# Short filler matmuls in the front, and the loads of two sequence steps cut in two by partitions

## The chip, the core and the metric

The kernel runs on one core of one Trainium2 chip, as one launch. The metric is the device time of that launch in microseconds: the median over several runs, with all seven inputs in device memory at the start and the output back in device memory at the end.

Five engines work side by side and each follows its own list of instructions: TensorE (PE in the profile, with its weight loads as a row of their own, PEld), VectorE (DVE), ScalarE (ACT), GpSimd (POOL) and SyncE (SP). Sixteen DMA engines move data. SP and POOL only issue transfers to them.

## The reference, cut to what matters

A gated recurrence over 768 tokens, for 4 batches and 8 heads of width 48, and after it a two-layer network with a product of two projections:

```python
f = 1.0 / (1.0 + np.exp(-f_logit))
for t in range(S):
    state = f[:, :, t, :, None] * state + np.einsum('bhd,bhe->bhde', k[:, :, t], v[:, :, t])
    y[:, :, t] = np.einsum('bhd,bhde->bhe', q[:, :, t], state)
x = y.transpose(0, 2, 1, 3).reshape(B * S, H * D)       # 3072 x 384
gate = np.maximum(x @ w_gate, 0.0)                      # 384 -> 1536
out = (gate * (x @ w_val)) @ w_out                      # 1536 -> 384
```

`q`, `k`, `v` and `f_logit` are 4 x 8 x 768 x 48 in float32, so for one head the 48 numbers of a token (192 bytes) lie together, and the tokens of a head follow one another.

## The kernel before

**Tiling.** The sequence is cut into six steps of 128 tokens (`C = 128`, `NC = 6`), and the batches of a step go in two pairs. Within a step the recurrence is a masked product of queries and keys plus a carried state (one 48 x 48 block for each head and batch). For each step and pair the kernel:

- loads f, k, q and v, one transfer each (`load`, issued at line 487 on SP);
- takes exp and ln of f on ACT (lines 742 and 744; 585 and 586 in the first two steps), sums over tokens with a triangular matmul (751; 594 in the first two steps), and takes two exponentials of the sums (761 and 763; 608);
- multiplies k and q by them ("hats", lines 773 and 777 on POOL; 610);
- transposes the hats, as DMA transposes issued by SP (795) from step 2 on, and on TensorE (642) in the first two steps;
- forms scores (817; 667), masks them on DVE (827; 683), multiplies with v and with the carried state (852; 712 and 717), and copies the result into `xT` (881; 729);
- updates the state (900; 692), and runs the network over the 512 rows of the step: two projections (922), relu on ACT (928), product on DVE (932), the output projection (965), a copy (975), and a store issued by SP (979).

Steps 0 and 1 (`twos`) take two neighbouring tokens into one partition, so their loads are 128 partitions of 8 runs of 384 bytes. From step 2 on the loads are 128 partitions (tokens) of 16 runs (heads of two batches) of 192 bytes.

**What sets the order.** Every instruction is added to a list with an assumed cost, and a planner (`Plan.schedule`, with `settle` for eight rounds) walks it and fixes the order on each engine before the program is emitted. On the chip each engine follows its list in order and waits on semaphores. A transfer has a semaphore of its own for each buffer slot, and its reader waits for 16 counts for each transfer of the slot so far (`dma`, line 460). In the planner a load is a number of parts (`64 * (b1 - b0)`) of 13.5 or 23 ns. All loads, transposes and stores go through SP's one queue in list order. The nine weight loads (three parts each of `wg`, `wv`, `wo`) go through POOL's queue (line 508), and the last of `wo` stands in POOL's list behind hats and copies of step 1. SP holds a load back until the load three before it has landed (`flight = 3`).

**Filler matmuls.** Until the first loads are in, TensorE has nothing to do. The kernel fills gaps in TensorE's planned list up to planned time 15 us with matmuls on a tile of zeros, into a bank of PSUM that is kept free until then (lines 1013 to 1036). `zeros` is 128 x 512 and is cleared by DVE (line 447) before the first of them. The number in a gap follows from the planned length of the gap:

```python
        gap, each = op.start - at, 0.44 if at < 4.0 else 0.23
        if begun and op.start <= warm_until:
            for _ in range(int((0.9 if gap > 1.5 else 0.6) * gap / each)):
                busy.append((op, warm))
```

This gives 18 matmuls of 512 columns: one before the gaps are counted (line 1015) and 17 at line 1024, which stand as 1 ahead of the `pick` matmul (434), 7 ahead of the first sums (594), 6 ahead of the first transposes (642), 1 ahead of the first scores (667) and 2 ahead of the first products with v (712). Every one loads its weights anew, so a matmul is two instructions in TensorE's list.

Of the kernel before, what the change touches and what calls it, by code (L numbers as in the profile page):

```python
# [8 lines left out]
BF16 = mybir.dt.bfloat16  # L9
# [33 lines left out]
class Plan:  # L43
# [10 lines left out]
    def add(self, eng, emit, reads=(), writes=(), occ=0.5, lat=0.2, prio=0, opens=(), after=(), follows=()):  # L54
        op = Op(eng, emit, list(reads), list(writes), occ, lat, prio, opens, after, follows)
        op.idx = len(self.ops)
        self.ops.append(op)
        return op
# [244 lines left out]
def bass_hgrn2_outer__then__ffn_reglu_kernel(  # L303
# [8 lines left out]
    out: bass.AP,  # L312
):
    twos = (0, 1)
    pe_hats = {(0, 0), (0, 1), (1, 0), (1, 1)}
    by_pool = {(0, 0, 0, 1), (0, 1, 0, 1)}
    halves = {0: 6, 1: 4, 2: 6}
# [9 lines left out]
    B, H, S, D = q.shape  # L327
    C = 128
# [12 lines left out]
    sb = nc.alloc_sbuf_tensor  # L341
# [40 lines left out]
    mask2 = sb("mask2", [128, 2, 2, 64], BF16)  # L382
    ident = sb("ident", [128, 128], BF16)
    ones = sb("ones", [128, 1], BF16)
    zeros = sb("zeros", [128, 512], BF16)
    banks = [nc.alloc_psum_tensor(f"ps{i}", [128, 512], F32) for i in range(8)]

    pl = Plan({"bc": 2, "bc4": 4, "tp": 2, "s": 4, "y": 2, "kv": 2, "f": 4})
    add = pl.add
    gp, ve, sc, te, sy = nc.gpsimd, nc.vector, nc.scalar, nc.tensor, nc.sync  # L390
# [13 lines left out]
    def pool_t(n):  # L404
        return dict(occ=0.1 + n * 2.2 / 1000.0, lat=0.12)
# [7 lines left out]
    def fill(eng, name, ap, value, cols, prio, key=None):  # L413
        e = engine[eng]
        add(eng, lambda: e.memset(ap, value), [], [key or name], occ=0.07 + cols / (1090.0 if eng == "DVE" else 1020.0), prio=prio)
# [19 lines left out]
    for t, name, src, sname in ((upto, "upto", tri, "tri"), (below, "below", tris, "tris")):  # L435
        add("DVE", lambda t=t, src=src: ve.tensor_tensor(t[:], src[:], same.ap[:, 0:128], ALU.mult), [same, sname], [name],
            occ=0.25, prio=-19)
    add("DVE", lambda: ve.tensor_copy(pick2[:], same.ap[:, 0:128].rearrange("p (b t) -> p b t", b=2)[:, :, 0]), [same], ["pick2"],
        occ=0.1, prio=-19)
    for i, src, name in ((0, upto, "upto"), (1, below, "below"), (1, upto, "upto")):  # L440
        lo = [m for m in range(2) if not (i and (name == "upto") != (m == 1))]
# [2 lines left out]
            src[:, 64:128].unsqueeze(1).to_broadcast([128, len(lo), 64]), ALU.add), [name], [f"mask2_{i}{m}" for m in lo],  # L444
            prio=-9, **pool_t(64 * len(lo)))

    fill("DVE", "zeros", zeros[:], 0.0, 256, -30)
    for i in range(NB):
        fill("DVE", f"bneg{i}", bneg[:, i], 0.0, 512, -28 if i < 1 else 11 if i < 2 else 30)
    for i in range(NH):  # L450
# [9 lines left out]
    def dma(op, slot, flow, parts, n=1):  # L460

        if slot not in slots:
            slots[slot] = [nc.alloc_semaphore(f"d_{slot}"), 0]
        slots[slot][1] += 16 * n
        op.sem, op.goal = slots[slot]
        op.flow, op.parts = flow, (n * parts[0], *parts[1:])

    srcs = {"f": f_logit, "k": k, "q": q, "v": v}

    def slot_of(n, c, pr):  # L470
        return (2 * c + pr) % NL[n]

    def in_keys(n, c, b0, b1):
        return [f"{n}{slot_of(n, c, b // 2)}_{b % 2}" for b in range(b0, b1)]

    def load(n, c, b0, b1, after=()):
        last = tails.get("load")
        t = ld[n]
        both, one = c in twos, b1 - b0 == 1
        if both:  # L480
            src = bass.AP(tensor=srcs[n].tensor, offset=(2 * c + b0 // 2) * H * S * D, ap=[[2 * D, C], [S * D, H], [1, 2 * D]])
            dst = bass.AP(tensor=t, offset=slot_of(n, c, b0 // 2) * 2 * HD, ap=[[NL[n] * 2 * HD, 128], [2 * D, H], [1, 2 * D]])
        else:
            src = bass.AP(tensor=srcs[n].tensor, offset=b0 * H * S * D + c * C * D,
                          ap=[[D, C], [S * D, (b1 - b0) * H], [1, D]])
            dst = t[:, slot_of(n, c, b0 // 2), b0 % 2:b0 % 2 + b1 - b0, :, :].rearrange("p b h d -> p (b h) d")
        op = add("SP", lambda: sy.dma_start(dst, src), [], in_keys(n, c, b0, b1),  # L487
                 occ=0.45 if both else 0.7 if one else 1.0, lat=0.9, prio=c * 100, after=after,
                 follows=[last] if last else [])
        tails["load"] = op  # L490
        dma(op, f"{n}{slot_of(n, c, b0 // 2)}" + f"_{b0 % 2}" * one, 0.95 * (b1 - b0),
            (64, 19, 27, 2.4) if both else (64 * (b1 - b0), 13.5, 23))
        return op

    WJ = NJ // wsteps
# [2 lines left out]
    def load_w(nm, s, after):  # L498
        if nm == "wo":
            src = bass.AP(tensor=w_out.tensor, offset=s * WJ * 128 * DM,  # L500
                          ap=[[DM, 128], [128 * DM, WJ], [1, DM]])
            dst = wo[:, s * WJ:(s + 1) * WJ, :]
        else:
            src = bass.AP(tensor=wsrc[nm].tensor, offset=s * WJ * 128,
                          ap=[[DFF, 128], [128 * DFF, NK], [1, WJ * 128]])
            dst = (wg if nm == "wg" else wv)[:, :, s * WJ * 128:(s + 1) * WJ * 128]
        last = tails.get("load_w")
        op = add("POOL", lambda: gp.dma_start(dst, src), [], [f"{nm}{s}"], occ=0.8, lat=1.2, prio=50, after=after,
                 follows=[last] if last else [])
        tails["load_w"] = op  # L510
        dma(op, f"{nm}{s}", 2.45, (32, 62, 80, 2.2) if nm == "wo" else (24, 80, 80, 2.6))
        return op

    loads, done, firsts = [], {}, []
    for item in first:
        item, _, behind = item.partition("@")
        gate = [done[behind]] if behind else []
        if item[0] == "w":
            op = load_w(item[:2], int(item[2:]), gate)
        else:  # L520
            c, b = int(item[1]), int(item[3])
# [464 lines left out]
    for c in range(NC):  # L986
        for b in range(0, B, 2):
            for n in "fkqv":
                if f"{n}{c}.{b // 2}" not in done:
                    loads.append(load(n, c, b, b + 2, loads[-flight:][:1]))  # L990
        for b in range(0, B, 2):
            if c in twos:
                attention_pair(c, b)
            else:
                attention_front(c, b)
                attention_front(c, b + 1)
                attention(c, (b, b + 1))
        for b0, b1, js in groups.get(c, [(0, 4, range(NJ))]):
            len0, js = len(pend), list(js)
            for at, j in enumerate(js):  # L1000
                ffn_hidden(c, b0, b1, j)
                if pend and c > 0 and (len(js) - 1 - at) / len(js) * len0 < len(pend):
                    ffn_out(*pend.pop(0))
            if c > 0 and js[-1] == NJ - 1:
                pend += [(c, [b]) for b in range(b0, b1)]
        if c == 0:
            for b in range(0, B, 2):
                ffn_out(0, [b, b + 1])
    for item in pend[:-1]:
        ffn_out(*item)  # L1010
    ffn_end(NC - 1, B - 1, [(0, 256), (256, DM)])

    WARM = 512
    warm_until = 15.0
    add("PE", lambda: te.matmul(banks[-1][:, 0:WARM], zeros[:, 0:128], zeros[:, 0:WARM]), ["zeros"], ["warm"], occ=0.2,
        prio=-30)
    for e in pl.ENGINES:
        pl.free0[e] = 0.8
    spare = banks[-1]
    order = pl.settle([(bk, warm_until if bk is spare else 0.0) for bk in banks], rounds=8, early=set(firsts))  # L1020
    waits = pl.needs()

    def warm():
        return te.matmul(spare[:, 0:WARM], zeros[:, 0:128], zeros[:, 0:WARM], start=True, stop=True, skip_group_check=True)

    busy, at, begun = [], pl.free0["PE"], False
    for op in order["PE"]:
        gap, each = op.start - at, 0.44 if at < 4.0 else 0.23
        if begun and op.start <= warm_until:
            for _ in range(int((0.9 if gap > 1.5 else 0.6) * gap / each)):  # L1030
                busy.append((op, warm))
        begun = True
        at = op.start + op.occ
    fillers = {}
    for op, emit in busy:
# [2 lines left out]
    for e in ("PE", "ACT", "DVE", "POOL"):  # L1038
        n = 0
# [75 lines left out]
```

## Time and profile before

| | before |
|---|---|
| time, median of 3 runs | 193.62 us (192.35 to 194.12) |
| span of the profiled run | 190.5 us |
| PE busy | 183.2 us, 96% |
| DVE, ACT, POOL busy | 105.1, 109.5, 76.2 us |
| moved by DMA | 32.04 MB in 108854 packets |
| of it on SP's queue | 28.19 MB in 104848 packets |
| f, k, q and v loads, issue to landing (median) | 5.6, 5.6, 5.1, 5.4 us |

A DMA share of 1.00 in the tables by stage means that on average each of the 16 engines had one packet under way; it goes over 1 where packets of one engine overlap. In a list of instructions the first number is the start from the beginning of the span, the second the time, "x16" the number of instructions merged into the line, and what stands in brackets is the idle time of the engine ahead of it and what ended that.

### The profile page before, as it was taken

To read this page: it belongs to the slowest core of one execution; us is meant where nothing else is said; L and a number is where in the kernel's file an instruction comes from. 1 tells how busy PE (TensorE), PEld (TensorE's weight loads), DVE (VectorE), ACT (ScalarE), POOL (GpSimd) and SP (SyncE) were. 2 spreads that over 40 slices of the span, in tenths; PEclk is the share of its full clock that TensorE was granted. 3 is DMA by queue.
4 is the path that set the end of the run, shared out by engine and by line. 5 is a ranking of instruction groups with operands and counts; after the bars stand their busy time and mean duration, and the time that the engine had idled before them with its cause. 6 is when DMAs were issued, how large, how long until landed. Compare 5 with 4: busy or idle time off the path is not lost.

```text
span 190.5 us, 5030 instructions
## 1 busy us (share of the span) xinstructions
PE 183.2 (96%) x2079; PEld 108.1 (57%) x2079; DVE 105.1 (55%) x189; ACT 109.5 (57%) x244; POOL 76.2 (40%) x109
## 2 busy tenths in 40 slices
PE   7988799999999999999999999999999999999995
PEld 2457584556685466768545564454555555554564
DVE  7699465994555866518695374625538233343300
ACT  3775459735698486575967739466533533334322
POOL 8497404771376638445393473715400000000000
PEclk9999999999999999999999999999999999999999
DMA  6999999999999999999999998999640310011113
GB/s 164 323 264 203 192 298 237 200 230 195 256 215 154 222 162 223 252 193 252 158 217 141 208 217 167 229 195 229 124 114 29 86 41 27 14 45 41 41 53 112
DMA packets 108854, 32.04 MB, mean 168 GB/s; under 512 B 101792, under 2 KB 108832, under 8 KB 108832
## 3 DMA queue, kind: packets, MB, share of 16 engines
q1 hardware_dynamic: 104848, 28.19, 73.2%
q0 software_dynamic: 3984, 3.54, 11.9%
q8 instruction: 16, 0.26, 0.6%
q14 instruction: 6, 0.05, 0.1%
HBM read 25.95 MB, written 4.72 MB: 161 GB/s over the span
## 4 chain that ended last, share of the span: by engine, by line
PE 73%; DMA 13%; ACT 4%; DVE 3%; SPq 2%; POOL 2%; issue 2%
PE ps L922 41%; PE ps L965 19%; DMA f_in<-in_f_logit_dram 8%; DMA wo<-in_moe_w_out_dram 5%; PE ps L852 2%; PE ps L817 2%; PE ps L751 1%; DVE qkT L650 1%; POOL hats L610 1%; PE ps L594 1%; SPq L487 1%; PE ps L900 1%; PE ps L945 1%; PE ps L667 1%; ACT f_in L742 1%
## 5 line engine op out<-in xcount | busy, mean ns | idle before, releaser
L932 DVE TENSOR_TENSOR gT<-relu,ps 128x512 bf16<-128x512 bf16 (+1 forms) x88 | 51.0, 587 | 61.2 <-PE ps L922 38.3
L928 ACT ACTIVATE relu<-ps 128x512 bf16<-128x512 f32 (+1 forms) x88 | 45.4, 521 | 27.6 <-PE ps L922 27.2
L922 PE MATMUL ps<-xT,wv 128*128 128x512 bf16 (+1 forms) x264 | 61.2, 340 | 0.0
L922 PE MATMUL ps<-xT,wg 128*128 128x512 bf16 (+1 forms) x264 | 61.1, 340 | 0.0
L965 PE MATMUL ps<-wo,gT 128*128 128x384 bf16 x276 | 49.0, 326 | 0.3 <-DMA wo<-in_moe_w_out_dram 0.3
L965 PEld LDWEIGHTS ps<-wo,gT 128*128 128x128 bf16 x276 | 26.2, 98 | 18.3 <-DMA wo<-in_moe_w_out_dram 0.4
L922 PEld LDWEIGHTS ps<-xT,wg 128*128 128x128 bf16 x264 | 24.8, 98 | 19.7 <-issue 1.6
L922 PEld LDWEIGHTS ps<-xT,wv 128*128 128x128 bf16 x264 | 25.0, 98 | 19.2
L975 ACT ACTIVATE osb<-ps 128x384 f32<-128x384 f32 x23 | 11.2, 494 | 26.2 <-PE ps L965 26.2
L827 DVE TENSOR_TENSOR ptm<-ps,tri 128x512 bf16<-128x512 f32 x32 | 20.4, 682 | 5.3 <-PE ps L817 5.2
L773 POOL TENSOR_TENSOR hats<-k_in,expo 128x384 bf16<-128x384 f32 x16 | 15.8, 998 | 17.7 <-ACT expo L761 15.3
L570 POOL TENSOR_TENSOR st<-ssum,dec 128x384 bf16<-128x384 f32 x16 | 13.1, 832 | 23.0 <-DVE ssum L568 22.9
L777 POOL TENSOR_TENSOR hats<-q_in,expo 128x384 bf16<-128x384 f32 x16 | 15.7, 998 | 4.4 <-DMA q_in<-in_q_dram 4.3
L568 DVE TENSOR_TENSOR ssum<-ps,st 128x384 f32<-128x384 f32 x16 | 8.4, 552 | 3.7 <-PE ps L900 3.5
L683 DVE TENSOR_TENSOR ptm<-ps,mask 128x512 bf16<-128x512 f32 x14 | 8.7, 680 | 1.5 <-PE ps L667 1.5
L761 ACT ACTIVATE expo<-ps 128x384 f32<-128x384 f32 x16 | 7.9, 494 | 2.8 <-PE ps L754 2.7
L763 ACT ACTIVATE expo<-ps 128x384 f32<-128x384 f32 x16 | 8.0, 501 | 0.0
L807 POOL CAST vpad<-v_in 128x384 bf16<-128x384 f32 x16 | 7.6, 507 | 0.4 <-DMA v_in<-in_v_dram 0.2
L742 ACT ACTIVATE f_in<-f_in 128x768 f32<-128x768 f32 x8 | 6.7, 842 | 1.5 <-DMA f_in<-in_f_logit_dram 1.5
L729 ACT ACTIVATE xT<-ps 128x384 bf16<-128x384 f32 x8 | 4.2, 599 | 5.8 <-PE ps L717 5.8
L744 ACT ACTIVATE bneg<-f_in 128x768 bf16<-128x768 f32 x8 | 6.7, 843 | 0.1
L881 ACT ACTIVATE xT<-ps 128x384 bf16<-128x384 f32 x12 | 5.2, 486 | 2.5 <-PE ps L852 2.5
(85 smaller groups left out, 163.4 us busy)
## 6 DMA issues: line engine op xcount, KB each, us to landing
f_in<-in_f_logit_dram SPq DMA_DIRECT2D x12, 384.0 KB, 5.6
k_in<-in_k_dram SPq DMA_DIRECT2D x12, 384.0 KB, 5.6
q_in<-in_q_dram SPq DMA_DIRECT2D x12, 384.0 KB, 5.1
v_in<-in_v_dram SPq DMA_DIRECT2D x12, 384.0 KB, 5.4
out_dram<-osb SPq DMA_DIRECT2D x23, 192.0 KB, 2.4
wg<-in_moe_w_gate_dram POOLq DMA_DIRECT2D x3, 384.0 KB, 5.5
wv<-in_moe_w_val_dram POOLq DMA_DIRECT2D x3, 384.0 KB, 6.2
wo<-in_moe_w_out_dram POOLq DMA_DIRECT2D x3, 384.0 KB, 8.8
```

Source lines behind the costliest of these rows:

```text
L568: add("DVE", lambda: ve.tensor_tensor(tmp[:, :], kv.ap[:, 0:HD], s_old[:, :], ALU.add), [kv, f"S{b}_{(c + 1) % 2}"], [key], prio=P + 8, ** ...
L570: add("POOL", lambda: gp.tensor_tensor(t4(s_new), t4(tmp), rate, ALU.mult), [key] + dk, [f"S{b}_{c % 2}"], prio=P + 8, **pool_t(HD))
L683: add("DVE", lambda i=i, j=j, mask=mask: ve.tensor_tensor(ptm[ms[i]][:, j, :, :], s[i][j].ap[:, :].rearrange("p (n t) -> p n t", n=NP), ma ...
L742: add("ACT", lambda: sc.activation(fl, fl, AF.Exp, scale=-1.0), keys, keys, prio=P, **act_t(2 * HD))
L773: add("POOL", lambda: gp.tensor_tensor(hk, kin[:, b % 2, :, :], ex[:, 1, :].rearrange("p (h d) -> p h d", h=H), ALU.mult), in_keys("k", c, ...
L777: add(e, lambda: engine[e].tensor_tensor(hq, qin[:, b % 2, :, :], ex[:, 0, :].rearrange("p (h d) -> p h d", h=H), ALU.mult), in_keys("q", ...
L827: add("DVE", lambda mi=mi, j=j, s=s: ve.tensor_tensor(ptm[mi][:, j, :, :], s.ap[:, :].rearrange("p (n t) -> p n t", n=NP), mask, ALU.mult) ...
L922: mm = te.matmul(bank.ap[:, 0:n], wt[:, kt, j * 128:(j + 1) * 128], xT[xi][:, kt, n0:n1], start=(kt == 0), stop=(kt == NK - 1))
L928: add("ACT", lambda: sc.activation(relu[ri][:, 0:n], gate.ap[:, 0:n], AF.Relu), [gate], [f"relu{ri}"], prio=P, **act_t(n))
L932: add("DVE", lambda: ve.tensor_tensor(gT[gi][:, j, n0:n1], relu[ri][:, 0:n], val.ap[:, 0:n], ALU.mult), [val, f"relu{ri}"], [f"gT{gi}_{j}_ ...
L965: mm = te.matmul(o[b].ap[:, 0:DM], gT[gi][:, j, b * C:(b + 1) * C], wo[:, j, :], start=(j == 0), stop=(j == NJ - 1))
L975: add("ACT", lambda b=b, oi=oi: sc.activation(osb[oi][:, :], o[b].ap[:, 0:DM], AF.Copy), [o[b]], [f"osb{oi}"], prio=P, **act_t(DM))
```

## The change

Two edits that have nothing to do with each other.

**Fillers.** The formula is replaced by a list written out. The first five gaps over 0.4 us in TensorE's planned list get 18 matmuls of 64 columns, 58 of 64, and 8, 3 and 5 of 128. The first matmul is 128 columns wide in place of 512. That is 93 matmuls in place of 18. They stand at the same five places. `zeros` shrinks to 128 x 128, so its clearing does too. The purpose is to keep TensorE's array busy with pieces that are short, so that a filler never holds up a real matmul for long.

**Loads.** Each f, k, q and v load of steps 3 and 4 becomes two transfers, over partitions 0 to 119 and 120 to 127 for f, 0 to 103 and 104 to 127 for k, 0 to 71 and 72 to 127 for q, 0 to 87 and 88 to 127 for v. Both are issued one after the other in the place of the one, on the same semaphore, and the reader waits for 32 counts. The bytes and the runs of 192 bytes are the same. The purpose is to spread the transfers differently over the DMA engines.

The order of the instructions on PE, DVE, ACT and POOL is otherwise that of before, apart from three clearings of `dec` on DVE that move together. On SP it is that of before with 16 more transfers.

```diff
+    parted = (3, 4)
...
-    zeros = sb("zeros", [128, 512], BF16)
+    zeros = sb("zeros", [128, 128], BF16)
...
-    fill("DVE", "zeros", zeros[:], 0.0, 256, -30)
+    fill("DVE", "zeros", zeros[:], 0.0, 64, -30)
...
         if both:
...
+            ends = [(src, dst)]
         else:
-            src = bass.AP(tensor=srcs[n].tensor, offset=b0 * H * S * D + c * C * D,
-                          ap=[[D, C], [S * D, (b1 - b0) * H], [1, D]])
-            dst = t[:, slot_of(n, c, b0 // 2), b0 % 2:b0 % 2 + b1 - b0, :, :].rearrange("p b h d -> p (b h) d")
-        op = add("SP", lambda: sy.dma_start(dst, src), [], in_keys(n, c, b0, b1),
+            cut = (0, {"f": 120, "k": 104, "q": 72, "v": 88}[n], C) if c in parted else (0, C)
+            ends = [(bass.AP(tensor=srcs[n].tensor, offset=b0 * H * S * D + c * C * D + lo * D,
+                             ap=[[D, hi - lo], [S * D, (b1 - b0) * H], [1, D]]),
+                     t[lo:hi, slot_of(n, c, b0 // 2), b0 % 2:b0 % 2 + b1 - b0, :, :].rearrange("p b h d -> p (b h) d"))
+                    for lo, hi in zip(cut, cut[1:])]
+        op = add("SP", lambda: [sy.dma_start(dst, src) for src, dst in ends], [], in_keys(n, c, b0, b1),
...
-            (64, 19, 27, 2.4) if both else (64 * (b1 - b0), 13.5, 23))
+            (64, 19, 27, 2.4) if both else (64 * (b1 - b0) // len(ends), 13.5, 23), len(ends))
...
-    WARM = 512
-    warm_until = 15.0
-    add("PE", lambda: te.matmul(banks[-1][:, 0:WARM], zeros[:, 0:128], zeros[:, 0:WARM]), ["zeros"], ["warm"], occ=0.2,
-        prio=-30)
+    add("PE", lambda: te.matmul(banks[-1][:, 0:128], zeros[:, :], zeros[:, :]), ["zeros"], ["warm"], occ=0.1, prio=-30)
...
-    def warm():
-        return te.matmul(spare[:, 0:WARM], zeros[:, 0:128], zeros[:, 0:WARM], start=True, stop=True, skip_group_check=True)
+    def warm(n):
+        return te.matmul(spare[:, 0:n], zeros[:, :], zeros[:, 0:n], start=True, stop=True, skip_group_check=True)
...
-    busy, at, begun = [], pl.free0["PE"], False
+    busy, at, short = [], None, [(64, 18), (64, 58), (128, 8), (128, 3), (128, 5)]
     for op in order["PE"]:
-        gap, each = op.start - at, 0.44 if at < 4.0 else 0.23
-        if begun and op.start <= warm_until:
-            for _ in range(int((0.9 if gap > 1.5 else 0.6) * gap / each)):
-                busy.append((op, warm))
-        begun = True
+        gap = op.start - at if at is not None else 0.0
+        if short and gap > 0.4:
+            n, many = short.pop(0)
+            busy += [(op, lambda n=n: warm(n))] * many
         at = op.start + op.occ
```

More of the change, by code (lines that the diff above doesn't have):

```diff
@@ L1019, in bass_hgrn2_outer__then__ffn_reglu_kernel @@
     spare = banks[-1]
-    order = pl.settle([(bk, warm_until if bk is spare else 0.0) for bk in banks], rounds=8, early=set(firsts))
+    order = pl.settle([(bk, 15.0 if bk is spare else 0.0) for bk in banks], rounds=8, early=set(firsts))
     waits = pl.needs()
-    def warm():
-        return te.matmul(spare[:, 0:WARM], zeros[:, 0:128], zeros[:, 0:WARM], start=True, stop=True, skip_group_check=True)
-    busy, at, begun = [], pl.free0["PE"], False
+    def warm(n):
+        return te.matmul(spare[:, 0:n], zeros[:, :], zeros[:, 0:n], start=True, stop=True, skip_group_check=True)
+    busy, at, short = [], None, [(64, 18), (64, 58), (128, 8), (128, 3), (128, 5)]
     for op in order["PE"]:
-        gap, each = op.start - at, 0.44 if at < 4.0 else 0.23
-        if begun and op.start <= warm_until:
-            for _ in range(int((0.9 if gap > 1.5 else 0.6) * gap / each)):
-                busy.append((op, warm))
-        begun = True
+        gap = op.start - at if at is not None else 0.0
+        if short and gap > 0.4:
+            n, many = short.pop(0)
+            busy += [(op, lambda n=n: warm(n))] * many
         at = op.start + op.occ
```

## The prediction

> **What bounds the kernel now.** I read the page first. TensorE is busy nearly all of the span, and the DMA share stands at its ceiling for two thirds of it:
>
> ```profile
> PE 183.2 (96%) x2079; PEld 108.1 (57%) x2079; DVE 105.1 (55%) x189; ACT 109.5 (57%) x244; POOL 76.2 (40%) x109
> DMA  6999999999999999999999998999640310011113
> q1 hardware_dynamic: 104848, 28.19, 73.2%
> q8 instruction: 16, 0.26, 0.6%
> ```
>
> So two resources are nearly full at once up to about 135 us: PE, and the stream of transfers. After that PE is alone. The table by stage shows it where the changed loads are issued (steps 3 and 4 are issued from 60.9 to 105.4 us):
>
> ```profile
> 76.00:82.00 6.00, 6.00 (x98) 4.23 (x97) 3.00 (x7) 3.38 (x7) 2.66 (x5) 1.00 1.32 220
> 94.00:100.00 6.00, 6.00 (x75) 2.98 (x76) 4.97 (x9) 4.41 (x12) 4.57 (x6) 1.00 1.33 216
> 112.00:118.00 6.00, 6.00 (x88) 3.37 (x87) 2.77 (x5) 4.57 (x9) 1.93 (x3) 1.00 0.86 179
> ```
>
> The last three columns are clock, DMA share and GB/s. PE has no idle time, and the DMA share is 1.3 until about 112 us and 0.9 after. A busy PE says that a faster stream of loads can't help here. Whether a slower one hurts depends on the slack between them, and two more views say that it is small. The chain runs through loads of step 5, and POOL starts on k and q when they land:
>
> ```profile
> 108.95 5.82 DMA f_in<-in_f_logit_dram
> 119.48 6.45 DMA f_in<-in_f_logit_dram
> ...
> POOL hats L777 <- DMA q_in<-in_q_dram: 4.3, 4, 1.1
> POOL hats L773 <- DMA k_in<-in_k_dram: 2.2, 1, 2.2
> ```
>
> The slack itself: the pair's transposed hats must have landed before its scores (817) run. From the landing records and PE's list: step 2, second pair, 71.87 against 73.75 us; step 3, 83.69 against 85.40 and 93.57 against 95.10; step 4, 106.98 against 108.00 and 119.22 against 120.05. That is 1.9, 1.7, 1.5, 1.0 and 0.8 us.
>
> For the front I read PE and PEld in order of time:
>
> ```profile
> 2.44 3.17 PE L1024 MATMUL ps<-zeros 128*128 128x512 bf16 x7
> 6.01 0.50 PE L594 MATMUL ps<-bneg,upto 128*128 128x384 bf16 x1 [0.41 <-ACT bneg L586]
> 7.52 1.47 PE L1024 MATMUL ps<-zeros 128*128 128x512 bf16 x6
> 8.89 0.92 PEld L642 LDWEIGHTS ps<-ident,hats 128*128 128x128 bf16 x16 [0.39 <-DVE hats L610]
> 22.19 0.22 PE L717 MATMUL ps<-qkT,st 128*32 128x128 bf16 x1 [1.32 <-issue]
> ```
>
> The fillers hold nothing up. The first sums wait for ACT, the first transposes for DVE's hats. Seven fillers take 3.17 us (about 0.43 each) and six later ones 1.47 us (0.22 in steady flow): the array runs at half rate until about 7.4 us. At 20.9 us PE stops for 1.32 us and nothing that the profile shows releases it.
>
> [...] a transfer runs on k engines[...]. For 128 partitions k is 16. The trace agrees as far as it goes: the sixteen counts of a load come within some 0.2 us (k at 95.22 to 95.36). It has no transfer with another partition count, so the case that matters is not shown. [...] instructions come in blocks of 16 KiB[...]. Queue q8 agrees: 16 packets, 0.26 MB.
>
> **The change, part by part.**
>
> Loads. A load of 128 partitions by 16 runs is 2048 packets, 128 for each engine. Where loads follow each other (first counts at 75.17, 77.01 and 78.74 us) one takes 1.78 us, 13.9 ns a packet: the engines are bound by packets. By the rule above the new transfers use k = 15 and 8 (f: 120 and 8 partitions), 13 and 12 (k: 104 and 24), 12 and 14 (q: 72 and 56), 11 and 10 (v: 88 and 40). [...] In packets that is 144, 160, 160 and 192, together 656 against 512, while the last engine gets none. A set of four loads then takes 144 more packets at 13.9 ns, 2.0 us more on the busiest engines, and there are four sets. A reader waits for the slowest engine, and a transpose queued behind the loads has its share on those same engines.
>
> How far behind the stream is at each use: step 2's second pair has f and k ahead of it, 48 packets, 0.7 us, inside its slack of 1.9. Step 3, first pair: six loads, 192 packets, 2.7 us less slack 1.7, PE stalls 1.0. Second pair: 304 packets, 4.2 less 1.5, 2.7 in all. Step 4, first pair: 480 packets, 6.7 less 1.0, 5.7 in all. Second pair: 576 packets, 8.0 less 0.8, 7.2 in all. These are totals, as a PE that stopped earlier comes later to the next use. After 112 us the share of 0.86 leaves room that takes up part of the last growth, and some windows before it are not full either (1.03 from 70 to 76). I take 5.2 us, with 2.7 and 7.2 as ends. On SP the 16 more issues cost 0.4 to 0.6 us each, from its shortest rows (0.37 and 0.58), 6 to 9 us over 45 us. That lies in time in which SP waits for room in its queue (its load issues there last 1.4 to 2.3 us), so I cost it at nothing. Behind each stand transposes that PE waits for, hence up to 0.5 us at the high end.
>
> Fillers ahead of the first sums. At half rate 512 columns take 0.43 us, so 64 take 0.053, and 18 take 1.0, 58 take 3.1 us. They end at about 5.6 us, as those of before do, and the sums start at 6.01 when ACT is done: 0. The unknown is whether a weight load for each 64 columns fits into 0.053 us. The nearest row is the eight 2-column matmuls at line 619, which with their weight loads take 0.26 us (7.26 to 7.52), 0.03 each; the other end is the 0.15 us that a weight load lasts at half rate, which would end the 58 at 11 us and cost 5. I take the first, as weight loads overlap matmuls.
>
> Fillers later. 8, 3 and 5 at 0.056 us (half of half the 0.22) are 0.45, 0.17 and 0.28 us in place of 1.3, 0.2 and 0.4. All sit in waits for DVE or POOL: gain 0 to 0.1. The shorter clearing of `zeros` frees DVE 0.2 us at 1 us, ahead of clearings with time to spare: 0.
>
> Instruction fetch. 75 more matmuls with their weight loads are 150 instructions, so every later block boundary moves 150 instructions ahead. If the stop at 20.9 us is a late block, it can vanish. What that is worth is limited: the next projections need the last third of `wv`, which lands at 25.08 us and is used at 25.30, so PE gains 0.2. The moved boundaries can also stop PE elsewhere. I take -0.2, from -1.7 to +1.
>
> Sum: 193.6 - 0.2 + 5.2 = 198.6 us.
>
> **The rivals.**
> 1. The split leaves the sixteen engines evenly loaded (k or the choice of engines is other than I read), or the delay is hidden. For it: no transfer here shows the rule. Against it: the rule, and slacks under 2 us. 193.6 - 0.2 = 193.4, no change.
> 2. Faster. The loads are even and both stops that look like fetches (1.32 at 20.9 and 0.40 us at 42.6) go, and the weights come early enough: 193.6 - 1.3 - 0.4 - 0.2 = 191.7. Against it: the landing at 25.08, and PE waits 0.26 us for `wo` at 44.82, whose landing at 44.77 no filler moves.
> 3. The loads are even, [...] the transposes, state updates and scores there (1.1, 0.5, 0.6 us) double in part, +1.3, 194.9. Against it: the sums before are dense.
>
> **How the numbers follow.** Chances: the skewed engines 0.50, rival 1 0.28, rival 2 0.12, rival 3 0.10. The first gives 196.1 to 201.1 with its ends. The range is 192.2 to 200.8: it leaves out most of rival 2 and the top of the first. Slower by over 1% (over 195.5): nearly all of the first and a bit of the third, 0.52. Faster by over 1% (under 191.7): most of the second, with the spread of rival 1 (before ran from 192.35 to 194.12), 0.12. The rest, 0.36, within 1%.
>
> **What would show it.** If I am right on the loads, the sixteen counts of a split load come far apart, the median landing of f, k, q and v rises by 1 us or more, PE shows idle time ahead of 817 between 85 and 121 us that grows by step, and q1 takes no more packets than before. If rival 1 holds, landings stay near 5.5 us. For the fillers: the sums start at 6.0 us, the transposes at 8.8 to 8.9, and the 0.22 us rate is reached by 7.5. If the stop at 20.9 us is a fetch, it moves or goes. Wrong would make me: [...] weight loads that hold the short fillers up.

## The result, and the profile after

| | before | after |
|---|---|---|
| time, median of 4 runs | 193.05 us (192.35 to 194.12) | 201.65 us (200.72 to 202.82) |
| span of the profiled run | 190.5 us | 199.0 us |

The kernel became slower: ratio 1.0444, 95% interval 1.0363 to 1.0524, or 8.6 us. Here and below a ratio comes from undisturbed runs alone, while a median is over all runs, so the two can stand a little apart.

The page of after, the lines that answer to those shown of before:

```profile
PE 182.6 (92%) x2137; PEld 111.6 (56%) x2154; DVE 105.2 (53%) x189; ACT 110.1 (55%) x244; POOL 76.0 (38%) x109
DMA  6999999998999999989999999999942201111113
q1 hardware_dynamic: 104972, 28.19, 72.7%
q8 instruction: 17, 0.28, 0.6%
```

PE works as long as before (182.6 against 183.2 us) in a span that is 8.5 us longer: the loss is idle time of PE, not slower work. SP's queue moved the same 28.19 MB with 124 more packets. The table by stage (PE, PEld, DVE, ACT and POOL busy, granted clock, DMA share, GB/s) says where:

```profile
76.00:82.00 6.00, 5.80 (x96) 4.01 (x94) 3.06 (x7) 3.16 (x9) 3.96 (x6) 1.00 1.16 170
94.00:100.00 6.00, 5.32 (x54) 3.10 (x55) 3.11 (x6) 3.90 (x10) 2.37 (x4) 1.00 1.16 180
112.00:118.00 6.00, 4.97 (x45) 2.66 (x47) 2.60 (x5) 4.46 (x13) 2.00 (x2) 1.00 1.07 173
```

PE has idle time in every row where before had none. In the first two rows the last column fell from 220 and 216 to 170 and 180 GB/s. In one window from 76 to 124 us PE is busy for 40.56 us of 48; before it was 48.00. That is 7.4 of the 8.5 us.

PE's list from 60 to 140 us, the lines with more than 0.2 us of idle time ahead of them (the bracket names what ended it):

```profile
87.50 0.62 PE L821 MATMUL ps<-qkT 48*128 48x128 bf16 x16 [1.19 <-DMA qkT<-hats]
94.36 0.80 PE L904 MATMUL ps<-vpad,hats 128*128 128x96 bf16 x8 [1.64 <-POOL vpad L811]
108.49 0.80 PE L904 MATMUL ps<-vpad,hats 128*128 128x96 bf16 x8 [2.11 <-POOL vpad L811]
112.88 0.34 PE L755 MATMUL ps<-bneg,tri 128*128 128x384 bf16 x1 [1.00 <-ACT bneg L748]
121.17 0.34 PE L904 MATMUL ps<-vpad,hats 128*128 128x96 bf16 x4 [0.45 <-POOL vpad L811]
```

(Line numbers after step 0 are four higher than before: 821 are the scores, 904 the state update, 755 the sums over tokens.) The longest stops stand ahead of the state update, which waits for POOL's copy of v, and POOL itself waited for loads. POOL's waits, in all, times, longest:

```profile
POOL hats L781 <- DMA q_in<-in_q_dram: 9.3, 7, 3.6
POOL hats L777 <- DMA k_in<-in_k_dram: 5.2, 1, 5.2
POOL vpad L811 <- DMA v_in<-in_v_dram: 5.1, 5, 1.7
```

Before, POOL waited 0.2 us for v and 4.3 for q. So late loads are the cause at first sight. They follow each other more slowly: in step 4 the whole sets of before landed 1.8 us apart (q 97.24, v 99.01, f 100.83), the split sets of after 2.9 us (k 102.08, q 104.40, v 107.87, f 110.75, k 113.63).

The front of after, PE in order of time:

```profile
2.45 2.79 PE L1025 MATMUL ps<-zeros 128*128 128x64 bf16 x58
5.97 0.34 PE L598 MATMUL ps<-bneg,upto 128*128 128x384 bf16 x1 [0.73 <-ACT bneg L590]
6.83 0.61 PE L1025 MATMUL ps<-zeros 128*128 128x128 bf16 x8
8.53 1.08 PE L646 MATMUL ps<-ident,hats 128*128 128x128 bf16 x16 [1.09 <-DVE hats L614]
18.09 1.03 PE L671 MATMUL ps<-qkT 48*64 48x128 bf16 x32 [0.78 <-DVE qkT L654]
```

The fillers hold nothing up, and the sums run at full rate (0.17 us each where before took about 0.3). But the 32 score matmuls at 18.09 take 1.03 us where before took 0.64: the half rate is back for 3.4 us (granted clock 0.51 from 18.09 to 21.49 us), after stops of 1.29 and 0.78 us. In the 3.4 us ahead of it PE had worked for 1.36 us. What sets the rate isn't shown. The last q load of step 0 came late in this profile: its last count is at 15.24 us where before had 12.71, and POOL waited 1.4 us for it. Why it came late isn't shown. The mean granted clock of all four runs of after, 0.982 to 0.992, would fit one or two such stretches in each, by my estimate: 3.4 us at half rate are 0.009 of 199 us. It need not be the new fillers' doing: E8 and E10 below, whose front is that of before, have it at 18.7 and 19.4 us, after stretches as idle (1.46 and 1.66 us of work in 3.4). At 53 us PE stands 0.4 us behind before.

### The profile page after: what moved, and what is told of

The parts are those of the page before. It is cut to its first block, busy times and chain, and to the rows that moved or that the text cites. A ratio compares the mean times of both kernels' runs of the same rounds, so it can differ in the third digit from the quotient of the medians.

```text
span 199.0 us, 5178 instructions
## 1 busy us (share of the span) xinstructions
PE 182.6 (92%) x2137; PEld 111.6 (56%) x2154; DVE 105.2 (53%) x189; ACT 110.1 (55%) x244; POOL 76.0 (38%) x109
## 3 DMA queue, kind: packets, MB, share of 16 engines
q1 hardware_dynamic: 104972, 28.19, 72.7%
## 4 chain that ended last, share of the span: by engine, by line
PE 60%; SPq 22%; DMA 12%; issue 1%; DVE 1%; POOL 1%; ACT 1%; DVEq 0%
PE ps L926 32%; PE ps L969 19%; SPq L491 17%; DMA v_in<-in_v_dram 8%; SPq L799 4%; DMA q_in<-in_q_dram 4%; POOL vpad L811 1%; PE ps L671 1%; PE ps L716 1%; PE ps L949 1%; PE ps L646 1%; PE ps L856 1%; PE ps L821 1%; PE ps L755 1%; PE ps L598 1%
## 5 line engine op out<-in xcount | busy, mean ns | idle before, releaser
L926 PE MATMUL ps<-xT,wg 128*128 128x512 bf16 (+1 forms) x249 | 58.6, 342 | 0.7 <-issue 0.2
L926 PEld LDWEIGHTS ps<-xT,wv 128*128 128x128 bf16 x264 | 25.3, 99 | 19.5 <-issue 0.2
L926 PEld LDWEIGHTS ps<-xT,wg 128*128 128x128 bf16 x264 | 25.1, 99 | 18.5
L781 POOL TENSOR_TENSOR hats<-q_in,expo 128x384 bf16<-128x384 f32 x16 | 15.7, 999 | 9.3 <-DMA q_in<-in_q_dram 9.3
L904 PE MATMUL ps<-vpad,hats 128*128 128x96 bf16 x48 | 3.9, 208 | 4.6 <-POOL vpad L811 4.2
L885 ACT ACTIVATE xT<-ps 128x384 bf16<-128x384 f32 x12 | 5.2, 488 | 3.2 <-PE ps L856 3.2
```

What stands on the lines that cost most here:

```text
L781: add(e, lambda: engine[e].tensor_tensor(hq, qin[:, b % 2, :, :], ex[:, 0, :].rearrange("p (h d) -> p h d", h=H), ALU.mult), in_keys("q", ...
L926: mm = te.matmul(bank.ap[:, 0:n], wt[:, kt, j * 128:(j + 1) * 128], xT[xi][:, kt, n0:n1], start=(kt == 0), stop=(kt == NK - 1))
```

## The experiments

What was to be told apart: theory S (skew, the prediction's): a set waits for the engines that carry most packets. Against it: theory P, each further transfer has a price of its own; theory K, a transfer over fewer than 16 engines is slow by itself, beyond its packets; theory F, the front (PE's first 30 us or so, where the fillers stand) makes the loss.

How many engines a transfer uses can be counted. In the trace every load leaves one packet of 4 bytes on each engine that it uses (in E5 below 16 for whole sets, 15 for 120 rows, 8 for eight rows). SP's queue has 1808 of them before and 1932 after. The prediction has 15+8, 13+12, 12+14 and 11+10 engines for the four pairs of a set, 95 in place of 64: 31 more, times four sets, is 124. That is exact, and it is also all of the 124 packets. The trace of before did not show these numbers, as every load there writes sixteen counts. That of after has them set by set: in step 4's first pair k has 13 of the 4-byte packets from 100.44 to 100.62 us and 12 from 100.98 to 101.14, v 11 from 105.25 to 105.43 and 10 from 106.22 to 106.46, q 26 in all and f 23. Which of the sixteen engines they are no trace shows.

### One part of the change alone

E1, the fillers alone:

```diff
-    parted = (3, 4)
+    parted = ()
```

> The kernel after with every load whole again: the 93 short fillers alone. Skew theory [...]: within 1 us of before, between 192.5 and 194.0, and PE idle between 84 and 122 us is gone. Front theory (the loss starts in the front, where the last q load of step 0 lands 2.5 us later and the half rate comes back at 18 us): at least half of the loss stays, 197 us or more.

Measured: 192.81 us beside 191.78 of before, ratio 1.0031 (1.0009 to 1.0054). Theory F falls. PE's list shows what became of the gain. After the front the 256-column projections end about 1.0 us ahead of before (the first 512-column group starts at 26.63 against 27.59 us), the stop at 20.9 us is gone, and then:

```profile
35.72 0.62 PE L646 MATMUL ps<-ident,hats 128*128 128x128 bf16 x8 [0.51 <-DVE hats L614]
38.12 0.64 PE L671 MATMUL ps<-qkT 48*64 48x128 bf16 x32 [0.57 <-DVE qkT L654]
85.82 0.62 PE L821 MATMUL ps<-qkT 48*128 48x128 bf16 x16 [0.45 <-DMA qkT<-hats]
```

PE's lead over before ends at waits for DVE that PE, coming earlier, now meets. At the scores of 62.67 us (62.80 before) little is left, and at 85.8 us a wait of 0.45 us for transposed hats takes it: the scores there start 0.4 us after those of before (85.40).

E2, the loads alone (the fillers as before, `parted = (3, 4)`):

> The fillers of before, and the split loads of the change alone. Skew theory and theory of a price for each transfer alike: 200.5 to 202.5, PE stops ahead of the state update, the scores and the sums of steps 3 and 4. Front theory: under 197.

Measured: 201.81 us beside 191.78 of before, ratio 1.0498 (1.0438 to 1.0558). The split makes the whole loss. As the front is that of before here, the delay of PE can be read off step by step, from the starts of the scores in PE's lists:

| scores of | before | E2 | behind | the prediction's total |
|---|---|---|---|---|
| step 2, second pair | 73.75 | 73.54 | -0.2 | 0 |
| step 3, first pair | 85.40 | 87.34 | 1.9 | 1.0 |
| step 3, second pair | 95.10 | 99.33 | 4.2 | 2.7 |
| step 4, first pair | 108.00 | 115.38 | 7.4 | 5.7 |
| step 4, second pair | 120.05 | 128.41 | 8.4 | 7.2 |
| step 5, first pair | 131.36 | 139.47 | 8.1 | |

### The price of a transfer, and the number of engines

E3 and E4 on top of E2, all four tensors cut alike (the other lines of the edit are those of E2, here and in E6 to E11, or follow from the lines shown):

```diff
-            cut = (0, {"f": 120, "k": 104, "q": 72, "v": 88}[n], C) if c in parted else (0, C)
+            cut = (0, 64, C) if c in parted else (0, C)        # E3
+            cut = (0, 120, C) if c in parted else (0, C)       # E4
```

> The fillers of before; the 16 loads of steps 3 and 4 in two transfers of 64 partitions each, so that each transfer has sixteen engines and no engine gets more than in before. Skew theory: as before, 192.5 to 194. Theory that each of the 16 added transfers costs its time on SP or in the stream: 199 or more.

> The fillers of before; all 16 loads cut at 120 and 8 partitions (15 and 8 engines), so the busiest engines get 16 packets more for each load, 256 in all against 576 in the change. Skew theory: a stream 3.6 us longer less a slack of about 1 us, 195 to 197. Theory that a transfer on fewer than sixteen engines has a price of its own on SP [...]: as in the change, 200 or more.

Measured: E3 194.54 us, 1.0135 (1.0086 to 1.0184), in neither of its two stretches but near the first. E4 200.51 us, 1.0439 (1.0385 to 1.0494). E4 lies well over what the packets say: its busiest engines carry 144 a set against 128, 0.22 us at 13.9 ns, yet its sets land 2.8 us apart (k 102.06, q 104.92, v 107.73, f 110.55), 1.0 more than whole ones. S alone does not explain that. That there is skew can be seen in the counts of E4's v set: 7 of the 15 engines of its first part report from 106.34 to 106.56 us, the other 8 from 107.24 to 107.31, and the 8 of its second part from 107.62 to 107.73. This is as it must be if eight engines carry both parts and run behind the rest. SP's list of E4, two transfers to a line:

```profile
98.59 2.41 SPq L491 DMA_DIRECT2D q_in<-in_q_dram  x2
101.04 2.77 SPq L491 DMA_DIRECT2D v_in<-in_v_dram  x2
103.86 2.88 SPq L491 DMA_DIRECT2D f_in<-in_f_logit_dram  x2
```

and of before, one to a line:

```profile
68.83 1.53 SPq L487 DMA_DIRECT2D q_in<-in_q_dram  x1
70.41 1.63 SPq L487 DMA_DIRECT2D v_in<-in_v_dram  x1
72.08 1.62 SPq L487 DMA_DIRECT2D f_in<-in_f_logit_dram  x1
```

SP is busy without a gap in both, so a set is accepted every 2.4 to 2.9 us in place of 1.6. The first transfer of a pair takes 0.33 us of it and the second, with 128 packets in all, 2.0 to 2.5: it is not long to issue (in E5 below, where eight rows go alone, such an issue takes 0.27 to 0.33 us), so I read it as waiting for room in the queue. SP's rule of holding a load until the third before it has landed doesn't bind here: f was issued at 103.86 us, and k, three before it, had landed at 102.06.

E6 moves E4's cut by eight rows, so that both parts divide by 16. The counts show 16 engines for 128 and 64 rows; for the 112 and 16 rows here, and the 48 and 32 of E8, I take it to be the same:

```diff
+            cut = (0, 112, C) if c in parted else (0, C)
```

> The front as before, all four tensors of steps 3 and 4 cut 112/16, so that both parts go over all 16 engines while the second is nearly as narrow as the 8 rows of the cut 120/8. Theory A (price of fewer than 16 engines): near the cut in halves, 194.0 to 196.0 us. Theory B (many engines into few partitions): near the cut 120/8, 198.5 to 201.5. Theory C (packets by engine): no more than the halves, 193.5 to 195.

Measured: ratio 1.0091 (1.0050 to 1.0132), median 195.36 beside 193.72. Its second part is nearly as narrow as E4's and its transfers as many. What is taken away is the number of engines below 16, and with it the skew (128 packets on each engine in place of 144 on the busiest). Four fifths of the loss go with them; E6 does not tell the two apart. Its sets land about 2.0 us apart (k 99.06, q 101.13, v 103.16). Theory B of that text, narrow parts, falls.

E7 takes even and odd partitions, E8 three parts of 48, 48 and 32, taken to be over 16 engines too (each row is first partition, end, step):

```diff
+            rows = [(0, C, 2), (1, C, 2)] if c in parted else [(0, C, 1)]                     # E7
+            rows = [(0, 48, 1), (48, 96, 1), (96, C, 1)] if c in parted else [(0, C, 1)]      # E8
...
```

> The front as before, all four tensors of steps 3 and 4 loaded as even and odd partitions, 64 each, both over all 16 engines and all over the partitions. If the 1.35% of the halves is the price of 16 more transfers: 194 to 195.2 us, as the halves. If it came from two halves that each cover only half of the partitions: 192.0 to 193.2, within 0.6% of before.

> The front as before, the tensors of steps 3 and 4 as three transfers of 48, 48 and 32 partitions, each over all 16 engines. If each additional transfer has a fixed price: 16 more cost the halves 1.35%, 32 cost 2.4 to 3%, 196.5 to 198 us. If the sync engine's work was hidden and only becomes the bound at some length: more than in proportion, over 199. If nothing but skew costs: 193 to 195.

Measured: E7 1.0107 (1.0011 to 1.0202), E8 1.0299 (1.0230 to 1.0367). With E3 and E6, three cuts into two parts over all engines cost 0.9 to 1.35%, and a cut into three 3.0%. So theory P holds as a part: 16 more transfers cost some 2 us in this kernel in each of three shapes, and 32 cost 5.8. That is more than twice as much at face value, but E8's interval reaches down to 2.3%, so it may be in proportion. Whether the price lies in SP's issue or on the engines these runs don't tell apart: alone, in the table of E5 below, halves and 112/16 follow each other 0.1 to 0.25 us later than whole sets, which over 16 sets could be all of it, but even and odd partitions don't.

E9 and E10 take E4 apart. E9 has its first transfer alone and leaves out rows 120 to 127, so part of the computation works on old data; E10 has a whole one with an eight-row one behind it, into a spare place, so that eight engines carry 128 and 16 packets a set:

```diff
+            rows = [(0, 120, 1)] if c in parted else [(0, C, 1)]                              # E9
+                    for lo, hi, to in [(0, C, t[...])] + [(120, C, extra[...])] * (c in parted)]   # E10
...
```

> The front as before; every tensor of steps 3 and 4 is one transfer of rows 0 to 119 over 15 engines. Rows 120 to 127 are left out, so that part of the computation works on old data. It takes the cut 120/8 apart. If a transfer over 15 engines is slow by itself in this kernel (its packets took 20.5 ns alone, against 15.7 for the whole): 197 us or more, most of the 4.4% of the cut 120/8. If it is as good as a whole one (1.96 us from set to set alone, against 1.82, times 16 sets, less the slack of some 1 us): 192.5 to 195.

> The front as before; every tensor of steps 3 and 4 is loaded whole, and a second transfer reads eight of its rows again, into a spare place over 8 engines. It is the other part of the cut 120/8. [...] If the loss of the cut is the small transfer over 8 engines (its issue, its 16 packets on half of the engines, the gap it makes): 198 us or more. If it is the 15 engines: no more than the price of a transfer over all engines, 193.5 to 196.

Measured: E9 1.0131 (1.0055 to 1.0208), E10 1.0147 (1.0037 to 1.0257, from two runs of 194.70 and 196.93 us). By its ratio E10 lies where the 15 engines were to be the cause, and E9 lies where they were not (at 195.1 just over its upper end): neither part carries the loss alone. Together they come to 2.8% where E4 has 4.4. One reason can be slack, the time by which a load lands ahead of its use: each part alone is paid for out of the same slack. It need not be the only one. In step 4 E9's sets land 2.0 us apart (k 100.97, q 103.04, v 104.99), as they do alone in E5, E10's 2.4 (k 100.35, q 102.73, v 105.09), and E4's 2.8. Over the whole set's 1.8 that is 0.2 and 0.6, 0.8 in all, where the two together make 1.0. So theory K, in the form that 15 engines are slow by themselves, is worth some 0.2 us a set here. E11 looks at slack with steps, the change's cuts in step 4 only:

```diff
-    parted = (3, 4)
+    parted = (4,)
```

> The front as before, the change's cuts in step 4 alone, half of the split sets. If each split set costs the same: half of the 5.0% of both steps, 196 to 197.5 us. If the loads of step 3 only use up the lead that the queue has (the first stop in the steps with both is at 80 to 87 us), step 4 alone costs clearly less than half: 193.5 to 195.5. If the stops come from step 4 alone: over 199.

Measured: 196.07 us, 1.0165 (1.0073 to 1.0257), where both steps cost 4.98%. Half the sets cost a third of the time at face value, which fits that the first sets use up the slack and the later ones are paid in full. But the interval reaches the half (2.5%), so E11 alone doesn't show it; the table of E2, where the first loads cut cost nothing, speaks for it.

### The loads by themselves

E5 leaves the kernel as it was and adds rows of four sets after its last store:

```diff
             for op in stores:
                 e.wait_ge(op.sem, op.goal)
+            for i, rows in enumerate(shapes):
+                for j in range(4):
+                    for lo, hi, by in rows:
+                        e.dma_start(...).then_inc(alone, 16)
+                        total += 16
+                e.wait_ge(alone, total)
```

> The kernel before, unchanged up to its last store; after it the sync engine loads four f sets one behind the other in each of eleven ways, with nothing else running: whole; 120 and 8 partitions; 120 alone; 8 alone; 112/16; 104/24; 88/40; 72/56; 64/64; even and odd partitions; whole again. Its extra time has no meaning, the rows of these loads do. Theory A (a transfer on fewer than 16 engines has a price of its own in the queue or on the engines): 120 alone takes clearly longer than whole, over 2.4 us from one to the next where a whole set takes 1.8, and 112/16 stays near 64/64 at about 2.0. Theory B (many engines that write into few partitions get in each other's way): 8 alone takes over 1 us from one to the next although each engine has 16 packets, 112/16 is as slow as 120/8, near 2.8, and 120 alone is near whole at 1.9. Theory C (all is load of the engines in packets): 120/8 and 104/24 take 2.0 and 2.3 by the busiest engine, 112/16 and 64/64 1.8.

Measured, from the landing of the first set to that of the fourth, a third of it; beside it the 192-byte packets' mean duration and what the busiest engine's packets give at 13.9 ns:

| | from set to set, us | packet, ns | by packets, us |
|---|---|---|---|
| whole (first and last row) | 1.82, 1.79 | 15.7, 17.8 | 1.78 |
| even / odd | 1.82 | 15.3 | 1.78 |
| 112/16 | 1.93 | 19.2 | 1.78 |
| 120 alone (15 engines) | 1.96 | 20.5 | 1.78 |
| 64/64 | 2.04 | 20.2 | 1.78 |
| 72/56 | 2.26 | 17.2 | 2.22 |
| 120/8 | 2.28 | 19.5 | 2.00 |
| 104/24 | 2.36 | 19.9 | 2.22 |
| 88/40 | 2.75 | 19.4 | 2.67 |

The eight rows alone follow each other at about 0.4 us. So A and B of that text fall, and with nothing beside, theory S (its C) is nearly right: the busiest engine gives 2.22 to 2.67 for three of the change's four cuts and the measurement lies 0.04 to 0.14 above; for 120/8 it is 0.28. It also shows that the same engines are the busy ones from set to set: if the engines of cut loads changed in turn through all 16, each would carry 128 packets a set in the mean and every cut row would take 1.78. That packets count for more than bytes the front of before shows: loads of the same 384 KB land 1.2 us apart there, in 1024 packets of 384 bytes (10.24, 11.45 and 12.71 us), and 1.8 us apart in step 4, in 2048 of 192. What theory S leaves out are 0.1 to 0.3 us for most transfers that aren't spread over partitions as a whole one is: even and odd partitions, both spread over all 128, keep the whole set's 1.82 us, while two halves take 2.04. The cause of that no run here shows, nor why 15 engines with the same 128 packets each take longer than 16. The packets' mean duration doesn't tell it: it is 19.2 and 20.2 ns for 112/16 and 64/64 too, and packets overlap (the DMA share is 1.38 in E13's row of whole sets).

E12 put such rows (four sets with one of the four tensors each) into the tail, ahead of stores, while PE, ACT and DVE compute, and again behind the end:

```diff
+            if op in tail and tail.index(op) in (0, 2, 4, 6):
+                group(tail.index(op) // 2, shapes[tail.index(op) // 2])
```

> The kernel before, its loads whole. In its tail, while the other engines compute and its own loads are done, the sync engine loads four sets f, k, q, v in each of four ways ahead of a store: 120/8, whole, 120 alone, 88/40; and the same four again after the last store, with nothing else running. Its time has no meaning. With nothing running, from set to set: 1.8 us whole, 1.95 for 120 alone, 2.3 for 120/8, 2.75 for 88/40, as measured before with one tensor. If the 2.8 us of the cut 120/8 inside the steps comes from the computation beside it, it is there in the tail too, 2.6 to 2.9; if from the mix of four tensors, also with nothing running; if neither, both show 2.3, and it comes from the transposes and stores in the same queue.

Measured: issues of the sets of 120/8 follow in the tail at 1.7, 2.2 and 2.2 us and behind the end at 1.6, 2.0 and 2.2; 88/40 at 1.7, 2.6, 2.9 and 1.8, 2.5, 2.8. The same, so neither that computation nor the four tensors make the 2.8 of the steps.

E13, rows of twelve behind the end (the loop of E5 with `range(3)` around the four tensors):

> The kernel before, unchanged up to its last store; after it twelve sets in a row, f, k, q and v in turn, in each of five ways with nothing else running: whole, cut 120/8, the change's cuts (f 120/8, k 104/24, q 72/56, v 88/40), 120 alone, cut 64/64. Its time has no meaning. Inside the steps the sets of the cut 120/8 land 2.8 us apart, in rows of four alone 2.3. If the engines that carry two parts fall further behind the longer the row is: the later sets of the row of twelve land 2.6 us or more apart, and the sets of 120 alone stay at 2.0. If a long row is as good as a short one, 2.3 throughout, the rest comes from what runs beside the loads in the steps.

Measured, steady part of the row by the issues: whole 1.78, 120/8 2.36 to 2.39, the change's cuts 2.4 in the mean, 120 alone 2.02, 64/64 2.10. SP's list of E13, whole sets and then 120/8:

```profile
204.44 1.75 SPq L1094 DMA_DIRECT2D k_in<-in_k_dram  x1
206.22 1.75 SPq L1094 DMA_DIRECT2D q_in<-in_q_dram  x1
...
226.47 2.45 SPq L1094 DMA_DIRECT2D q_in<-in_q_dram  x2
228.96 2.31 SPq L1094 DMA_DIRECT2D v_in<-in_v_dram  x2
231.32 2.28 SPq L1094 DMA_DIRECT2D f_in<-in_f_logit_dram  x2
```

Each line fills its interval, as in the steps, which I read again as SP waiting for room: the first load of the row of whole sets, at 190.19 us with nothing ahead of it, is issued in 0.40 us, those at 204.44 and 206.22 in 1.75. The page of E13 bears out the counts of engines: SP's queue has 227509 packets, 122661 more than before. Of these, 121344 are the rows' 192-byte packets, and the other 1317 are what 16, 15+8, the change's 95 for four sets, 15 and 16+16 engines give. The row's length adds nothing after the first few sets. E14 puts one engine's work at a time beside such rows, all others idle:

```diff
+    beside = [(parts, ""), (parts, "POOL"), (parts, "DVE"), (parts, "ACT"), (parts, "PE"), (whole, "POOL"), (parts, "POOL DVE ACT PE")]
```

> The kernel before, unchanged up to its last store; after it seven rows of twelve sets: cut 120/8 with nothing beside; with products of 128x384 in float32 on GpSimd beside them; with the same on the vector engine; with exponentials on the scalar engine; with matmuls of 512 columns; whole sets with GpSimd's products; cut 120/8 with all four engines at work. Its time has no meaning. Cut 120/8 follows at 2.36 us with nothing beside, and at 2.8 inside the steps. If one engine's work makes the difference, its row stands at 2.6 us or more from set to set and the last row too; the whole sets with GpSimd then show whether they suffer as well (1.78 with nothing beside). If no row is over 2.45, the difference isn't in the engines' work on SBUF, and stays open.

Measured, from set to set: 2.39 with nothing, 2.35 beside POOL, 2.31 DVE, 2.36 ACT, 2.26 PE, 2.39 beside all four; whole sets beside POOL 1.81. No row is over 2.45 in the mean. The last 0.4 us of the 2.8 inside the steps stay open. Inside the steps the 192-byte packets of E4 take 26.7 ns from 98 to 108 us against 19 to 21 in these rows. In the same stretch they take 17.3 in before, 17.5 in E6, 18.5 in E9, 21.2 in E10 and 22.0 in E2. So fewer than 16 engines is not enough for it, as E9 has 15, and neither are eight engines with more packets, as E10 has them. It takes both parts of the cut inside the steps, and what makes it there these runs don't say. It is not transposes and stores issued between the loads: SP issued none between 96.8 and 109.6 us in E4.

## Why the prediction was wrong

Forecast 198.6 us with a range to 200.8; measured 201.65. The direction and the mechanism's first half were right, the size was not. Step by step:

**Loads, the engines.** Right. The numbers of engines taken give 124 more 4-byte packets, and 124 there are. The trace of before showed neither them nor that both parts of a load share engines, which the 144, 160, 160 and 192 packets need (9, 10, 10 and 12 rows of 16). The runs do: E5's rows follow the busiest engine, and E4's counts show the eight engines behind. Transposes write sixteen counts too, and they spread: from 97.12 to 98.49 us in after for one of step 3's, where before had 90.69 to 90.87. PE is idle ahead of 821 and 904 between 85 and 121 us, and the delay grows by step. Two of the signs named were bad ones. The counts of a split set do come far apart (1.8 us for a v set of step 4), but so do those of E3's evenly loaded halves (100.85 to 102.59 us): two transfers write to one semaphore. Nor do the counts of a whole load always come within 0.2 us: those of an f load of before come from 112.23 to 114.77. And the median from issue to landing was to rise by 1 us or more, but rose from 5.6, 5.6, 5.1 and 5.4 us only to 6.0, 6.1, 5.1 and 5.9 for f, k, q and v: where SP waits to issue, much of a set's delay stands ahead of its issue. That "q1 takes no more packets" missed by the 124.

**Loads, the size. This is the step that failed:** "A set of four loads then takes 144 more packets at 13.9 ns, 2.0 us more", and "I take 5.2 us, with 2.7 and 7.2 as ends". Measured is 9.6 us (the 4.98% of E2), and three terms were off:
- *The set of four.* The change's cuts alone with nothing beside take 2.4 us a set, 9.6 for four, against 7.1 whole: 2.5 more. Inside the steps four sets took 10.8 us (k at 101.62 to k at 112.41 in E2): 3.7 more, not 2.0. Of the 1.7 that are missing, 0.5 is in the table of E5, and 1.2 appears only inside the steps, with its cause open.
- *The discount.* The working had 7.2 us at step 4's second pair, and I took 5.2, on the ground that the DMA share of 0.86 after 112 us takes up part of the last growth. By then the stream was late, and that room was gone: the share from 112 to 118 us is 1.07 after. E2 stood 7.4 us behind one pair earlier and 8.4 there, and 8.1 in step 5: next to nothing was given back.
- *SP's 16 issues, costed "at nothing".* Cuts into two over all 16 engines, which add no packets to any engine but their last four bytes, cost 0.9 to 1.35% (E3, E6, E7), so 1.7 to 2.6 us. So more transfers weren't free, though SP had time in which it waited for room. Where the price arises is open, as said above.

The three overlap and don't add up. Of the 4.4 us between 5.2 and 9.6, the discount is 2.0 by the working's own total of 7.2. The table of E2 puts 1.2 at the size (8.4 beside 7.2). The other 1.2 is what lies between the profile and the medians: the profiled run of E2 was the fastest of its four (200.31 us, the median 201.81).

**Slack.** The slack of 1.9 to 0.8 us was read at the scores. The longest stops came at the state update (904), which needs v, for which no slack was worked out: 4.2 us of waits against 1.4 at the scores. That changes where PE stands still; for how long, by my reading, it changes little, since all sets pass the same queue.

**Fillers.** Right where they stand: sums at 5.97, transposes at 8.53 (8.81 in E1), full rate before 7.5. When the full rate begins varies, for a reason that isn't shown: it is at 4.5 us in after and 6.6 in E1, but with the fillers of before anywhere from 4.3 (E4) to 7.6 (before). The 58 short ones took 2.79 us in after and 3.27 in E1, with 3.1 worked out, so the weight loads do fit. Rival 3 let the half rate last longer with 1.0 us less of fillers between 7.5 and 9 us; that fewer fillers prolong it no trace shows. A half rate came in the profile of after, at 18 us and not at 7.5, and not in E1's; as E8 and E10 have it with the old fillers, it doesn't speak for rival 3.

**Instruction fetch.** The stop at 20.9 us went, as said, and so did that at 42.6. In before, packets of 16 KB start on q8 at 19.85 and 40.84 us, ahead of them; that a late fetch made the stops isn't shown. The first such packet starts at 14.10 us in before and at 8.46 in after. The gain was to be 0.2 us; measured is a loss of 0.3%, some 0.6 us, within the -1.7 to +1 given.

**Rivals 1 and 2** needed evenly loaded engines. They are not, and E3, E6 and E7 show that even loading would not have given "no change" either.

## What to carry to other kernels

If the transfers' queue is full beside a full TensorE, cost a split by what a set takes from one to the next, not by its bytes: here whole 1.8 us, two parts over 16 engines 1.8 to 2.1, over fewer 2.3 to 2.8. Cut partitions so that each part divides by 16, or don't cut: 112/16 cost 0.9% where 120/8 cost 4.4%. And a delay in a full queue is carried from step to step (1.9, 4.2, 7.4 and 8.4 us behind in E2), so don't discount it by a room that the late stream itself will have used up.

## What was not expected of the hardware

- Eight partitions fewer made a transfer longer: 120 over 15 engines follow at 2.02 us, 128 over 16 at 1.78 (E13).
- Loads ended late by one of sixteen counts when an instruction fetch started ahead of or among their packets. In E1's front a fetch of 16 KB starts at 9.51 us, and the k, v and q loads there have 15 of 16 counts at 10.21, 11.41 and 12.66 us but the last at 11.75, 12.83 and 14.03. In before, with the first fetch at 14.10 us, the last counts came at 10.24, 11.45 and 12.71. With 150 more instructions in PE's list, the fetch comes while these loads are under way, and they end 1.3 to 1.5 us later; that the fetch delays them is my reading. The same is seen further on in before: a fetch starts at 112.43 us, and the f load under way has 15 counts at 112.96 and the last at 114.77.
